# Row maximum and scaling of attention scores in one VectorE operation, with the threshold kept in PSUM

## Chip, cores and metric

The program runs on one core of a Trainium2 chip. The metric is device time in microseconds (us) of one execution; lower is better. The names of the engines are those of the profile: PE (TensorE), DVE (VectorE), ACT (ScalarE), POOL (GpSimd) and SP, whose queue issues most DMAs.

## What is computed

Attention with a threshold, then a mixture of experts over its output. The change lies in the attention alone (batch 8, heads 8, sequence 576, head dimension 64):

```
scale = 1.0 / np.sqrt(q.shape[-1])                       # 0.125
scores = scale * np.matmul(q, k.transpose(0, 1, 3, 2))
thresh = np.max(scores, axis=-1, keepdims=True) - tau
scores = np.where(scores >= thresh, scores, -1000000000.0)
scores = scores - np.max(scores, axis=-1, keepdims=True)
attn = np.exp(scores)
attn = attn / (np.sum(attn, axis=-1, keepdims=True) + 1e-09)
out = np.matmul(attn, v)
```

Then each token of the output whose `x @ w_skip` is positive goes to the one of 8 experts with the highest gate value: `x + gate * (relu(x @ w1[e]) @ w2[e])`. Everything is fp32.

## The kernel before

Queries are taken in tiles of 128 rows. A group `g` is two heads of one batch (32 groups); it has 9 items (`STEP`): four query tiles of each head, and one item for the two remainders of 64 rows together. So 288 items run through the same steps, with their names in `plan_item`:

- `score` (PE, L686): two fp32 matmuls of 288 columns each, into two adjacent PSUM banks. Three such pairs are in use at a time (`SPB`), and a pair comes free only after `mask`.
- `top` (DVE, L691): the row maximum over the 576 scores, read from PSUM, into `mx[..0]`.
- `small` (DVE, L695): from the maximum, two numbers per row in one scalar_tensor_tensor whose two tensor inputs, `cd` and `cd` again, lie in SBUF: `max - 8*tau` (the threshold on unscaled scores) and `-0.125*max` (the bias).
- `expo` (ACT, L700): `exp(0.125*score + bias)` from PSUM into `p` in SBUF.
- `mask` (DVE, L706): `(score >= threshold) * p`, with the scores from PSUM and `p` from SBUF.

After the two items of a query tile, `fph` makes an fp16 copy `pk` of `p` (ACT or DVE, L510/L512), `fpl` the fp16 remainder (POOL, L737), and SP transposes `pk` by DMA into `pt` or `ptm`. PE then multiplies these by the values (L788, L792), a sum column gives the normalizer, POOL scales (L841), and PE and DVE work out the gate logits.

The order of all this on every engine is written by a planner (`Plan`): each step is given as an operation with its dependences, a due time and a cost, and the planner simulates the engines and sorts; a list of seeds (`SEEDS`) disturbs the order, and the last disturbed order is emitted. Where the planner sees PE idle, it puts in matmuls without use (`fill`, L518), as many as fit into the share `FILL` of the gap. An engine takes its instructions strictly in the order that was emitted. After the attention (up to about 750 us) come the experts, PE with weights streamed in, whose code isn't touched.

Of the kernel before, what the change touches and what calls it, by code (L numbers as in the profile page):

```python
# [12 lines left out]
F32 = mybir.dt.float32  # L13
# [4 lines left out]
AF = mybir.ActivationFunctionType  # L18
ALU = mybir.AluOpType
AX = mybir.AxisListType  # L20
# [4 lines left out]
P = 128  # L25
S = 576
# [8 lines left out]
HS = S // 2  # L35
# [15 lines left out]
STEP = 2 * NM + 1  # L51
NBK = 2 * NM + 1
SPB = 3
FILL = 0.7
SHB = 2
QB = 3
PFB = 4
# [21 lines left out]
SHARED = {"shp": 0, "gps": 0, "avp": 0, "sps": 2}  # L79
BANKS = 8  # L80
SEEDS = (
# [6 lines left out]
)  # L88
DLAT = 0.7
OFF = dict(  # L90
    ld=14.0, S=3.0, mx=2.4, sm=2.3, e=2.0, p=1.6, ph=0.6, phD=3.0, pl=0.4, tr=0.0, av=3.0, v=24.0, v0=20.0, ldv=-6.0, vsp=1.0, ld0=-30.0,
    init=6.0, row=2.0, rsp=0.5, L1=4.0, sc=0.0,
)

# [43 lines left out]
class Plan:  # L138
# [4 lines left out]
    def emit(self, o):  # L143
# [6 lines left out]
        if e == "PE" and o.real and o.idle[1] is not None:  # L150
            for _ in range(int(FILL * o.idle[0] / 0.115)):
                self.fill(o.idle[1])
# [218 lines left out]
def attn_moe_kernel(ctx: ExitStack, tc: tile.TileContext, qk, vl, tau, wg, w1, w2, out):  # L371
    nc = tc.nc
# [5 lines left out]
    cp = ctx.enter_context(tc.tile_pool(name="cp", bufs=1))  # L378
# [18 lines left out]
    taue = cp.tile([P, 1], F32, name="taue")  # L397
    nc.scalar.activation(taue, cnt[:, 0:1], AF.Exp)
    nc.vector.tensor_scalar(taue, taub, 0.0, None, op0=ALU.max)
    cd = cp.tile([P, 4], F32, name="cd")  # L400
    nc.gpsimd.memset(cd[:, 0:1], 1.0)
    nc.gpsimd.memset(cd[:, 1:2], -0.125)
    nc.gpsimd.memset(cd[:, 3:4], 0.0)
    nc.vector.tensor_scalar(cd[:, 2:3], taue, -8.0, None, op0=ALU.mult)
    jt = cp.tile([P, P], F32R, name="jt")
    onesr = cp.tile([1, P], F32, name="onesr")

# [77 lines left out]
    pl = Plan(tc)  # L485
    PE, DVE, ACT, POOL, SPQ = "PE", "DVE", "ACT", "POOL", "SP"
    BOTH = (DVE, POOL)

    def wtile(dt, name, n=1):
        return wraw.tile([P, n * WW], dt, name=name, tag="wr")  # L490
# [17 lines left out]
    def copy(e, dst, src):  # L508
        if e == ACT:
            nc.scalar.activation(dst, src, AF.Copy)  # L510
        else:
            nc.vector.tensor_copy(dst, src)  # L512

    ring = pl
# [6 lines left out]
    T = {}  # L521
# [143 lines left out]
    def sps():  # L665
        a, b = pl.bank
        return banks[:, a : b + 1 : b - a]

    def plan_item(g, i):
        n = STEP * g + i  # L670
        M = i == STEP - 1
        c, h = divmod(i, 2)
        ends = M or h == 1
        z = ("p", g, c)
        items = 1 if M else 2

        def two(t):
            return t.rearrange("p (a b) -> p a b", a=2)

        def score():  # L680
            T["S", g, i] = ps = sps()
            raw = T["raw", g]
            rs = slice(0, P) if M else slice(h * D, h * D + D)
            for j in range(2):
                ks = slice(QW + j * HS, QW + j * HS + HS)
                nc.tensor.matmul(ps[:, j, 0:HS], raw[rs, c * P : c * P + P], raw[rs, ks], start=True, stop=True)  # L686

        def top():
            if i == 0:
                T["mx", g] = ap_.tile([P, STEP, 4], F32, name="mx", tag="mx", bufs=3)  # L690
            nc.vector.tensor_reduce(T["mx", g][:, i, 0:1], T["S", g, i][:, :, 0:HS], AX.XY, ALU.max)  # L691

        def small():
            m = T["mx", g][:, i]
            nc.vector.scalar_tensor_tensor(m[:, 1:3], cd[:, 0:2], m[:, 0:1], cd[:, 2:4], op0=ALU.mult, op1=ALU.add)  # L695

        def expo():
            if h == 0:
                T[z] = ap_.tile([P, 2, S], F32, name="p", tag="p", bufs=PFB)
            nc.scalar.activation(  # L700
                two(T[z][:, h]), T["S", g, i][:, :, 0:HS], AF.Exp, bias=T["mx", g][:, i, 2:3], scale=0.125
            )

        def mask():
            e = two(T[z][:, h])
            nc.vector.scalar_tensor_tensor(  # L706
                e, T.pop(("S", g, i))[:, :, 0:HS], T["mx", g][:, i, 1:2], e, op0=ALU.is_ge, op1=ALU.mult
            )

        s = pl.op(n - OFF["S"], score, [T["q", g]] + ring.take("sps", SPB), {PE: 1.05 if M else 0.56})  # L710
        m = pl.op(n - OFF["mx"], top, [s] + (ring.take("mx", 3) if i == 0 else [T["m0", g]]), {DVE: 0.665})
        if i == 0:
            T["m0", g] = m
        m = pl.op(n - OFF["sm"], small, [m], {DVE: 0.13})
        e = pl.op(n - OFF["e"], expo, [m] + (ring.take("p", PFB) if h == 0 else T["es", g]), {ACT: 0.635})
        x = pl.op(n - OFF["p"], mask, [e], {DVE: 0.725})
        ring.free("sps", [x])
        T.setdefault(("Sop", g), []).append(s)
        T.setdefault(("es", g), []).append(e)
        T.setdefault(("ms", g), []).append(x)  # L720
        T.setdefault(("all", g), []).append(x)
        if M:
            ring.free("raw", T["Sop", g])
            ring.free("mx", T["all", g])
        if not ends:
            return
        ms, T["ms", g], T["es", g] = T["ms", g], [], []

        def fph(e):
            T["k", g, c] = ap_.tile([P, 2, 2 * S], F16, name="pk", tag="pk", bufs=KB)  # L730
            copy(e, T["k", g, c][:, 0:items, 0:S], T[z][:, 0:items])

        def fpl():
            k, p = T["k", g, c][:, 0:items], T.pop(z)[:, 0:items]
            for lo, w, at in ((0, NM * P, S + TL), (NM * P, TL, S)):
                ks = slice(lo, lo + w)
                nc.gpsimd.tensor_tensor(k[:, :, at : at + w], p[:, :, ks], k[:, :, ks], op=ALU.subtract)  # L737

        def turn():
            k = T.pop(("k", g, c))  # L740
            if M:
                T["pt", g, c] = PTM[g % MB]
                nc.sync.dma_start_transpose(T["pt", g, c][:, :, TL : TL + P], k[:, 0])
                return
            if c % 2 == 0:
                T["slot", g, c // 2] = wtile(F16, "pt", 2).rearrange("p (c a k q) -> p c a k q", c=2, a=2, q=P)
            T["pt", g, c] = pt = T["slot", g, c // 2][:, c % 2]
            nc.sync.dma_start_transpose(pt.rearrange("p a k q -> p (a k) q"), k.rearrange("p a b -> p (a b)"))

        w = items * S  # L750
        ph = pl.op(
            n - OFF["ph"],
            fph,
            ms + ring.take("pk", KB),
            {ACT: w / 1160 + 0.1, DVE: w / 1920 + 0.12},
            off={DVE: OFF["phD"]},
            port=BOTH,
        )
        lo = pl.op(n - OFF["pl"], fpl, [ph], {POOL: w * 0.00206 + 0.12})
        ring.free("p", [lo])  # L760
        q = ring.take("ptm", MB) if M else ring.take("wr", WRB) if c % 2 == 0 else [(T["tr", g, c - 1],)]
        t = T["tr", g, c] = pl.dma(n - OFF["tr"], turn, [ph, lo] + q, [0.35], 1.35 * items)
        ring.free("pk", [t])
        if M:
            for hd in range(2):
                plan_av(g, hd, n)
# [727 lines left out]
    for g in range(NG):  # L1494
        if g + 2 < NG:
            plan_load(g + 2)
        for i in range(STEP):
            t = STEP * g + i
            plan_item(g, i)
            while later and later[0][0] <= t:  # L1500
                later.pop(0)[1]()
        if g % HP == HP - 2 and g + 2 < NG:
            plan_v(g // HP + 1)
# [404 lines left out]
```

## Time and profile before

| | |
|---|---|
| runs before, median (lowest to highest) | 1059.12 us (1057.99 to 1062.39), 3 runs |
| the profiled execution's own time | 1049.39 us |
| its span, first to last instruction | 1047.6 us |
| granted TensorE clock, mean over the span | 0.905 |
| busy: PE, DVE, ACT, POOL | 93%, 74%, 55%, 59% of the span |

[...] PE's busy share contains the fill matmuls. All durations of the rows below come from the one profiled execution, which is about 10 us under the median of the three runs.

### The profile page before, as it was taken

How to read it: one execution, taken by the hardware profiler on the slowest of the kernel's cores; microseconds unless marked ns; L12 is line 12 of the kernel's file. 1: busy time of each engine (PE TensorE's matmuls, PEld its weight loads, DVE VectorE, ACT ScalarE, POOL GpSimd, SP SyncE). 2: the span in 40 equal slices, each digit the busy share in tenths (PEclk: the TensorE clock that was granted, in tenths of full speed). 3: DMA queues.
4: the chain of work that ended last, by engine and by line, in shares of the span. 5: the costliest groups of instructions: out<-in, count | busy, mean ns of one | idle time of the engine just before them, and what ended most of it. 6: DMA issues, size and time to landing. Idle time of an engine off the chain costs nothing. (4 is left out here: it accounts for less than half of the span.)

```text
span 1047.6 us, 21896 instructions
## 1 busy us (share of the span) xinstructions
PE 973.9 (93%) x8602; PEld 746.1 (71%) x8602; DVE 774.9 (74%) x1376; ACT 579.6 (55%) x872; POOL 617.8 (59%) x566
## 2 busy tenths in 40 slices
PE   7998999998989899899999999999988999999995
PEld 4666666766666676666656776666777989999994
DVE  7988698698679897968986788978645455557771
ACT  4766566666565676557656657645422434434450
POOL 4666575575466476656866576767715446444461
PEclk9999799699789898969987889977989999999998
DMA  6899697799579779958996689876943655344530
GB/s 177 170 194 151 119 234 155 131 208 202 106 160 177 177 143 229 182 105 165 181 207 140 152 202 167 156 156 116 191 152 124 214 181 160 129 164 175 191 126 17
DMA packets 371817, 169.79 MB, mean 162 GB/s; under 512 B 344270, under 2 KB 344270, under 8 KB 371712
## 3 DMA queue, kind: packets, MB, share of 16 engines
q1 hardware_dynamic: 367024, 158.72, 69.4%
q0 software_dynamic: 4544, 9.65, 2.9%
q8 instruction: 68, 1.11, 0.4%
q14 instruction: 37, 0.30, 0.1%
q10 hardware_dynamic: 144, 0.00, 0.0%
HBM read 69.46 MB, written 15.21 MB: 81 GB/s over the span
## 5 line engine op out<-in xcount | busy, mean ns | idle before, releaser
L737 POOL TENSOR_TENSOR pk<-p,pk 128x1024 f16<-128x1024 f32 (+1 forms) x320 | 366.8, 1170 | 230.6 <-issue 113.4
L686 PE MATMUL banks<-raw 64*128 64x288 f32 (+1 forms) x1152 | 377.4, 472 | 34.2 <-DVE p L706 32.1
L700 ACT ACTIVATE p<-banks,mx 128x576 f32<-128x576 f32 x288 | 210.2, 737 | 187.1 <-DVE mx L695 157.4
L691 DVE TENSOR_REDUCE mx<-banks 128x1 f32<-128x576 f32 x288 | 215.2, 751 | 113.6 <-PE banks L686 110.4
L686 PEld LDWEIGHTS banks<-raw 64*128 64x128 f32 (+1 forms) x1152 | 202.0, 207 | 115.0 <-DVE p L706 48.0
L706 DVE SCALAR_TENSOR_TENSOR p<-banks,mx,p 128x576 f32<-128x576 f32 x288 | 230.1, 807 | 8.6 <-ACT p L700 7.6
L510 ACT ACTIVATE pk<-p 128x1152 f16<-128x1152 f32 (+1 forms) x154 | 164.2, 1067 | 32.3 <-DVE p L706 21.0
L695 DVE SCALAR_TENSOR_TENSOR mx<-cd,mx 128x2 f32<-128x2 f32 x288 | 178.7, 625 | 2.4
L788 PEld LDWEIGHTS <-pt 128*128 128x128 f16 x2304 | 128.8, 104 | 26.7 <-issue 24.4
L518 PE MATMUL banks<-jt 128*128 128x256 f16 x874 | 138.3, 296 | 3.3 <-DVE p L706 2.2
L792 PE MATMUL banks<-Vl,pt 128*128 128x64 f16 x1280 | 139.2, 201 | 1.2 <-POOL Vl L645 1.2
L788 PE MATMUL banks<-Vh,pt 128*128 128x65 f16 x2304 | 139.8, 203 | 0.0
L518 PEld LDWEIGHTS <-jt 128*128 128x128 f16 x874 | 82.9, 105 | 68.7 <-issue 57.3
L792 PEld LDWEIGHTS <-pt 128*128 128x128 f16 x1280 | 122.8, 105 | 3.2 <-issue 0.5
L1542 POOL TENSOR_TENSOR wl<-wr,wh 128x1024 fp32r<-128x1024 f32 x28 | 72.4, 2603 | 35.3 <-ACT wh L1541 29.9
L1581 PE MATMUL hps<-xh,wl 128*128 128x256 f32 (+4 forms) x256 | 77.0, 301 | 0.0
L1581 PE MATMUL hps<-xh,wh 128*128 128x256 f32 (+4 forms) x248 | 76.4, 308 | 0.0
L1581 PE MATMUL hps<-xl,wh 128*128 128x256 f32 (+4 forms) x248 | 75.0, 302 | 0.0
L1582 ACT ACTIVATE HH<-hps 128x256 fp32r<-128x256 f32 (+4 forms) x64 | 27.0, 422 | 68.4 <-PE hps L1581 67.8
L1593 POOL DMA_INDIRECT out<-o,ids x21 | 21.1, 1006 | 72.0 <-DVE o L1592 28.9
L1541 ACT ACTIVATE wh<-wr 128x1024 fp32r<-128x1024 f32 x60 | 60.6, 1050 | 0.0
L1583 DVE SCALAR_TENSOR_TENSOR HH<-hps,HH 128x256 fp32r<-128x256 f32 (+4 forms) x64 | 31.1, 487 | 39.0 <-ACT HH L1582 38.9
(211 smaller groups left out, 1303.8 us busy)
## 6 DMA issues: line engine op xcount, KB each, us to landing
wr<-in_w SPq DMA_DIRECT2D x30, 1024.0 KB, 5.4
raw<-in_qk SPq DMA_DIRECT2D x32, 608.0 KB, 4.8
vraw<-in_vl SPq DMA_DIRECT2D x32, 320.0 KB, 4.2
out<-xb SPq DMA_DIRECT2D x32, 256.0 KB, 2.7
pt<-pk SPq DMA_TRANSPOSE x128, 5.2
rw<-in_w SPq DMA_DIRECT2D x2, 1024.0 KB, 6.4
out<-x SPq DMA_DIRECT2D x8, 128.0 KB, 2.8
lst<-rec,si POOLq DMA_INDIRECT x36, 3.9
```

The costliest lines, as they stand in the source:

```text
L510: nc.scalar.activation(dst, src, AF.Copy)
L518: nc.tensor.matmul(banks[:, n, 0 : 2 * P], x[:, 0:P], x[:, 0 : 2 * P], start=True, stop=True, skip_group_check=True)
L686: nc.tensor.matmul(ps[:, j, 0:HS], raw[rs, c * P : c * P + P], raw[rs, ks], start=True, stop=True)
L691: nc.vector.tensor_reduce(T["mx", g][:, i, 0:1], T["S", g, i][:, :, 0:HS], AX.XY, ALU.max)
L695: nc.vector.scalar_tensor_tensor(m[:, 1:3], cd[:, 0:2], m[:, 0:1], cd[:, 2:4], op0=ALU.mult, op1=ALU.add)
L700: nc.scalar.activation(two(T[z][:, h]), T["S", g, i][:, :, 0:HS], AF.Exp, bias=T["mx", g][:, i, 2:3], scale=0.125)
L706: nc.vector.scalar_tensor_tensor(e, T.pop(("S", g, i))[:, :, 0:HS], T["mx", g][:, i, 1:2], e, op0=ALU.is_ge, op1=ALU.mult)
L737: nc.gpsimd.tensor_tensor(k[:, :, at : at + w], p[:, :, ks], k[:, :, ks], op=ALU.subtract)
L788: nc.tensor.matmul(pv[:, c, :], x, Vh[:, vh, kt, :], start=(c + kt + i == 0), stop=False, skip_group_check=True)
L792: nc.tensor.matmul(pv[:, c, 0:D], x, Vl[:, vh, kt, :], start=False, stop=last, skip_group_check=True)
L1542: lo[q % 2].tensor_tensor(w[1][:, sl], rs, w[0][:, sl].bitcast(F32), op=ALU.subtract)
L1581: nc.tensor.matmul(hp_[:, 0:cap], w_, x, start=(i == 0), stop=(i == len(mm) - 1))
```

## The change

`top` becomes one tensor_tensor_reduce: it adds a zero tile, broadcast from one element in SBUF, to the scores, multiplies by -0.125, writes the result back over the scores in PSUM, and reduces by minimum with the accumulator output `mx[..1]`. That minimum is `-0.125*max`, so it is the bias of `expo` directly, and `expo` scales by -1. `small` becomes `minimum + tau`, one element per row, written to PSUM beside the scores (column 288 of the first bank), and `mask` compares with `<=` against it there. The planner's table changes with it: `expo` depends on `top` and no longer on `small`; `mask` depends on both. `FILL` goes from 0.7 to 0.5, and the seeds are others. The constants `cd` go, and a memset of one zero comes.

```
-FILL = 0.7
+FILL = 0.5
...
-    ld=14.0, S=3.0, mx=2.4, sm=2.3, e=2.0, p=1.6, ph=0.6, phD=3.0, pl=0.4, tr=0.0, av=3.0, v=24.0, v0=20.0, ldv=-6.0, vsp=1.0, ld0=-30.0,
+    ld=14.0, S=3.0, mx=2.4, th=2.1, e=2.0, p=1.6, ph=0.6, phD=3.0, pl=0.4, tr=0.0, av=3.0, v=24.0, v0=20.0, ldv=-6.0, vsp=1.0, ld0=-30.0,
...
-            nc.vector.tensor_reduce(T["mx", g][:, i, 0:1], T["S", g, i][:, :, 0:HS], AX.XY, ALU.max)
+            y = T["S", g, i][:, :, 0:HS]
+            nc.vector.tensor_tensor_reduce(
+                y, y, zero.broadcast_to([P, 2, HS]), -0.125, 3.0e38, ALU.add, ALU.min, T["mx", g][:, i, 1:2]
+            )
...
-            m = T["mx", g][:, i]
-            nc.vector.scalar_tensor_tensor(m[:, 1:3], cd[:, 0:2], m[:, 0:1], cd[:, 2:4], op0=ALU.mult, op1=ALU.add)
+            nc.vector.tensor_scalar(T["S", g, i][:, 0, HS : HS + 1], T["mx", g][:, i, 1:2], taue, None, op0=ALU.add)
...
-                two(T[z][:, h]), T["S", g, i][:, :, 0:HS], AF.Exp, bias=T["mx", g][:, i, 2:3], scale=0.125
+                two(T[z][:, h]), T["S", g, i][:, :, 0:HS], AF.Exp, bias=T["mx", g][:, i, 1:2], scale=-1.0
...
-                e, T.pop(("S", g, i))[:, :, 0:HS], T["mx", g][:, i, 1:2], e, op0=ALU.is_ge, op1=ALU.mult
+                e, ps[:, :, 0:HS], ps[:, 0, HS : HS + 1], e, op0=ALU.is_le, op1=ALU.mult
...
-        m = pl.op(n - OFF["sm"], small, [m], {DVE: 0.13})
-        e = pl.op(n - OFF["e"], expo, [m] + (ring.take("p", PFB) if h == 0 else T["es", g]), {ACT: 0.635})
-        x = pl.op(n - OFF["p"], mask, [e], {DVE: 0.725})
+        y, m = m, pl.op(n - OFF["th"], small, [m], {DVE: 0.13})
+        e = pl.op(n - OFF["e"], expo, [y] + (ring.take("p", PFB) if h == 0 else T["es", g]), {ACT: 0.635})
+        x = pl.op(n - OFF["p"], mask, [m, e], {DVE: 0.725})
```

What the built program makes of it on DVE, in the order of its queue, in the first third of the attention (`[waits X]` names the engine whose semaphore the instruction waits for; Activation is ACT). Before, three scores were reduced with their `small` steps between, and every `mask` waited for ACT:

```order
L706 SCALAR_TENSOR_TENSOR p<-banks,mx,p 128x576 [waits Activation_49]
L833 RECIPROCAL z<-z 128x10 [waits Activation_49]
L691 TENSOR_REDUCE mx<-banks 128x1 [waits PE_49]
L706 SCALAR_TENSOR_TENSOR p<-banks,mx,p 128x576 [waits Activation_49]
L695 SCALAR_TENSOR_TENSOR mx<-cd,mx 128x2 [waits DVE_49]
L691 TENSOR_REDUCE mx<-banks 128x1 [waits PE_49] x2
L695 SCALAR_TENSOR_TENSOR mx<-cd,mx 128x2 [waits DVE_49]
```

Of the change, near the same place (lines move by 8 to 10 up to L716, so `top` is L700, `small` L705, `expo` L710, `mask` L716):

```order
L716 SCALAR_TENSOR_TENSOR p<-banks,p 128x576 [waits Activation_49]
L700 ISA banks,mx<-banks,zero 128x2x288 [waits PE_49]
L700 ISA mx 128x1
L843 RECIPROCAL z<-z 128x10 [waits Activation_49]
L705 TENSOR_SCALAR banks<-mx,taue 128x1 [waits Activation_49]
L700 ISA banks,mx<-banks,zero 128x2x288 [waits PE_49]
L700 ISA mx 128x1
L716 SCALAR_TENSOR_TENSOR p<-banks,p 128x576 [waits DVE_49,Pool_49]
L705 TENSOR_SCALAR banks<-mx,taue 128x1 [waits Activation_49]
L705 TENSOR_SCALAR banks<-mx,taue 128x1 [waits DVE_49]
L716 SCALAR_TENSOR_TENSOR p<-banks,p 128x576 [waits DVE_49]
```

The one tensor_tensor_reduce is two DVE instructions, the pass over the scores and one that writes out the accumulator (`ISA mx`). `small` has moved behind the exponential in 157 of the 288 items: there it waits for ACT, since it writes into the bank that `expo` reads; in the others `expo` waits for it. In 70 places a `small` that waits for ACT stands directly in front of another `small`.

On PE, at the transpose for the value maximum of the fourth batch (`ident,vmx`), before; `jt` are the fill matmuls and `raw` the scores:

```order
L593 MATMUL banks<-ident,vmx 1x128 [waits DVE_49]
L686 MATMUL banks<-raw 128x288 [waits DVE_49]
L686 MATMUL banks<-raw 128x288
L518 LDWEIGHTS jt
L518 MATMUL banks<-jt 128x256 [waits Activation_49]
L686 MATMUL banks<-raw 128x288 [waits DVE_49]
```

Of the change:

```order
L601 MATMUL banks<-ident,vmx 1x128 [waits DVE_49]
L694 MATMUL banks<-raw 128x288 [waits DVE_49]
L694 MATMUL banks<-raw 128x288
L526 LDWEIGHTS jt
L526 MATMUL banks<-jt 128x256 [waits Activation_49]
L526 LDWEIGHTS jt
L526 MATMUL banks<-jt 128x256
L694 MATMUL banks<-raw 128x288 [waits DVE_49]
```

The fill matmuls stand at other places, and over the whole program there are 578 of them, where before there were 874. The number of DMAs and of POOL operations on data is the same in both.

## Rows read from the trace of the kernel before

**Rows 1.** Page, head: span of the profiled execution and its instructions

```profile
span 1047.6 us, 21896 instructions
```

**Rows 2.** Busy us by engine in two stages: attention and experts

```profile
core 0: us, PE busy (x) PEld busy (x) DVE busy (x) ACT busy (x) POOL busy (x), PEclk, DMA share, GB/s
0.00:750.00 750.00, 699.21 (x6640) 492.76 (x6641) 612.82 (x1111) 467.01 (x682) 480.09 (x475) 0.88 0.83 167
750.00:1048.00 298.00, 274.67 (x1962) 253.31 (x1961) 162.13 (x266) 112.56 (x191) 137.75 (x92) 0.96 0.46 149
```

**Rows 3.** Groups by line in 0 to 750 us: busy us, mean ns | idle before

```profile
L706 DVE SCALAR_TENSOR_TENSOR p<-banks,mx,p 128x576 f32<-128x576 f32 x288 | 230.1, 807 | 8.6 <-ACT p L700 7.6
L691 DVE TENSOR_REDUCE mx<-banks 128x1 f32<-128x576 f32 x288 | 215.2, 751 | 113.6 <-PE banks L686 110.4 <-ACT z L830 0.7 <-ACT p L700 0.5
L695 DVE SCALAR_TENSOR_TENSOR mx<-cd,mx 128x2 f32<-128x2 f32 x288 | 178.7, 625 | 2.4
...
L518 PE MATMUL banks<-jt 128*128 128x256 f16 x845 | 134.3, 296 | 3.3 <-DVE p L706 2.2 <-DVE lg L937 1.1
```

**Rows 4.** Waits in 0 to 750 us: total us, times, longest us

```profile
ACT p L700 <- DVE mx L695: 157.4, 118, 4.5
...
DVE mx L691 <- PE banks L686: 110.4, 112, 3.6
...
PEld banks L686 <- DVE p L706: 48.0, 55, 2.3
PE banks L686 <- DVE p L706: 32.1, 42, 2.1
```

**Rows 5.** Tile mx: ns min/median/max of its instructions

```profile
L695 DVE SCALAR_TENSOR_TENSOR mx<-cd,mx x288: 187/308/3793, 10.4 to 748.4; 128x2 f32<-128x2 f32 x144
...
L706 DVE SCALAR_TENSOR_TENSOR p<-banks,mx,p x288: 743/808/820, 11.6 to 749.7; 128x576 f32<-128x576 f32 x144
```

**Rows 6.** Timeline of DVE around 325 us: start us, length us

```profile
324.26 0.80 DVE L706 SCALAR_TENSOR_TENSOR p<-banks,mx,p 128x576 f32<-128x576 f32 x1
324.99 2.17 DVE L695 SCALAR_TENSOR_TENSOR mx<-cd,mx 128x2 f32<-128x2 f32 x1
```

**Rows 7.** Timeline of POOL in 324 to 327 us

```profile
325.01 2.13 POOL L737 TENSOR_TENSOR pk<-p,pk 128x1024 f16<-128x1024 f32 x1 [1.34 <-issue]
```

**Rows 8.** Timeline of all engines, 363.5 to 370 us

```profile
363.80 1.68 DVE L695 SCALAR_TENSOR_TENSOR mx<-cd,mx 128x2 f32<-128x2 f32 x1
...
365.40 2.25 DVE L706 SCALAR_TENSOR_TENSOR p<-banks,mx,p 128x576 f32<-128x576 f32 x3
365.57 0.74 ACT L700 ACTIVATE p<-banks,mx 128x576 f32<-128x576 f32 x1 [2.31 <-DVE mx L695]
...
366.26 1.23 PE L686 MATMUL banks<-raw 64*128 64x288 f32 x4 [1.76 <-DVE p L706]
```

**Rows 9.** Timeline of POOL in 364 to 365.4 us

```profile
363.34 2.12 POOL L737 TENSOR_TENSOR pk<-p,pk 128x1024 f16<-128x1024 f32 x1
```

**Rows 10.** Small DVE instructions by line: ns min/median/max

```profile
L598 DVE TENSOR_SCALAR vmx<-vmx x8: 141/142/143, 19.5 to 642.5; 1x1 f32<-1x1 f32 x8
L1039 DVE TENSOR_SCALAR gw<-gw x5: 158/161/336, 230.1 to 781.2; 128x9 f32<-128x9 f32 x3, 128x4 f32<-128x4 f32 x1, 128x5 f32<-128x5 f32 x1
L833 DVE RECIPROCAL z<-z x32: 194/205/216, 60.3 to 768.3; 128x10 f32<-128x10 f32 x32
```

**Rows 11.** Two-input DVE operations with (L1030) and without (L1102) a broadcast input

```profile
L1030 DVE TENSOR_TENSOR ca<-lg,gw x5: 181/223/224, 226.9 to 780.6; 128x72 f32<-128x72 f32 x3, 128x32 f32<-128x32 f32 x1, 128x40 f32<-128x40 f32 x1
L1102 DVE TENSOR_TENSOR ca<-ca x5: 186/232/233, 348.6 to 784.1; 128x72 f32<-128x72 f32 x3, 128x32 f32<-128x32 f32 x1, 128x40 f32<-128x40 f32 x1
```

**Rows 12.** Groups by line and shape: one DVE operation at two widths

```profile
L1583 DVE SCALAR_TENSOR_TENSOR HH<-hps,HH 128x256 fp32r<-128x256 f32 x24 | 10.1, 419 | 14.5 <-ACT HH L1582 14.5
...
L1583 DVE SCALAR_TENSOR_TENSOR HH<-hps,HH 128x384 fp32r<-128x384 f32 x8 | 4.4, 553 | 7.4 <-ACT HH L1582 7.4
```

**Rows 13.** Fill matmuls (L518) alone in stretches: busy us and count, granted clock

```profile
350.00:400.00 50.00, 8.50 (x59) 4.97 (x59) 1.00 0.79 155
450.00:500.00 50.00, 9.92 (x59) 5.83 (x60) 0.85 0.67 129
...
700.00:750.00 50.00, 16.02 (x97) 10.04 (x97) 0.83 0.82 156
```

More of the change, by code (lines that the diff above doesn't have):

```diff
@@ L399, in attn_moe_kernel @@
     nc.vector.tensor_scalar(taue, taub, 0.0, None, op0=ALU.max)
[L400 to L404, printed above, removed]
+    zero = cp.tile([P, 1, 1], F32, name="zero")
+    nc.vector.memset(zero, 0.0)
     jt = cp.tile([P, P], F32R, name="jt")
@@ L700, in expo @@
             nc.scalar.activation(
-                two(T[z][:, h]), T["S", g, i][:, :, 0:HS], AF.Exp, bias=T["mx", g][:, i, 2:3], scale=0.125
+                two(T[z][:, h]), T["S", g, i][:, :, 0:HS], AF.Exp, bias=T["mx", g][:, i, 1:2], scale=-1.0
             )
         def mask():
-            e = two(T[z][:, h])
+            e, ps = two(T[z][:, h]), T.pop(("S", g, i))
             nc.vector.scalar_tensor_tensor(
-                e, T.pop(("S", g, i))[:, :, 0:HS], T["mx", g][:, i, 1:2], e, op0=ALU.is_ge, op1=ALU.mult
+                e, ps[:, :, 0:HS], ps[:, 0, HS : HS + 1], e, op0=ALU.is_le, op1=ALU.mult
             )
         s = pl.op(n - OFF["S"], score, [T["q", g]] + ring.take("sps", SPB), {PE: 1.05 if M else 0.56})
-        m = pl.op(n - OFF["mx"], top, [s] + (ring.take("mx", 3) if i == 0 else [T["m0", g]]), {DVE: 0.665})
+        m = pl.op(n - OFF["mx"], top, [s] + (ring.take("mx", 3) if i == 0 else [T["m0", g]]), {DVE: 0.73})
         if i == 0:
             T["m0", g] = m
-        m = pl.op(n - OFF["sm"], small, [m], {DVE: 0.13})
-        e = pl.op(n - OFF["e"], expo, [m] + (ring.take("p", PFB) if h == 0 else T["es", g]), {ACT: 0.635})
-        x = pl.op(n - OFF["p"], mask, [e], {DVE: 0.725})
+        y, m = m, pl.op(n - OFF["th"], small, [m], {DVE: 0.13})
+        e = pl.op(n - OFF["e"], expo, [y] + (ring.take("p", PFB) if h == 0 else T["es", g]), {ACT: 0.635})
+        x = pl.op(n - OFF["p"], mask, [m, e], {DVE: 0.725})
         ring.free("sps", [x])
```

23 rows, old and new, of the table SEEDS are left out of this document.

## The prediction

> **What bounds the kernel now.** I read the stages first. The profiled execution spans 1047.6 us [rows 1] and took 1049.4; in the attention, its first 750 us, PE is busy for 699 us, DVE for 613, ACT for 467, POOL for 480 and the DMA engines for a share of 0.83 [rows 2]. The change touches only this stage; the experts' 298 us stay. Per item (288 of them) the stage takes 2.60 us. DVE works 613 / 288 = 2.13 us of it. PE works 699 - 134 = 565 us without its fill matmuls [rows 3], 1.96 us an item, and is idle for only 750 - 699 = 51 us. So no engine is full with real work; PE and DVE hand an item to and fro and wait for each other. The list of waits shows both directions: `top` waited 110 us for scores, and the scores' weight loads waited 48 us (the matmuls 32 us of the same moments) for a `mask` that frees a PSUM pair; ACT waited 157 us for `small`, but ACT has room [rows 4].
>
> Then I looked at DVE's three steps. `top` takes 751 ns and `mask` 807. `small`, two elements a row, takes 625 ns in the mean [rows 3], from 187 ns at best to 3793 ns at worst [rows 5]. The timelines tell why: at 324.99 us a `small` lasts 2.17 us, to 327.16, and POOL's subtraction, begun at 325.01, ends at 327.14 [rows 6, 7]; at 363.80 another lasts until 365.48, and POOL's ends at 365.46 [rows 8, 9]. A DVE operation with two inputs from SBUF is held until POOL's is done. `mask`, with one input from PSUM and one from SBUF, never goes over 820 ns beside the same POOL work [rows 5], so it isn't held.
>
> **The change part by part.**
>
> Removed: the holds. An unheld `small` is near 0.21 us (best 0.187), so of the 178.7 us, 178.7 - 288 x 0.21 = 118 us are holds [rows 3, 5]. The new `small` has one tensor input in SBUF and writes PSUM, and the new `top` reads one input from PSUM and one from SBUF as `mask` does; I expect neither to be held. Whether they are hasn't been seen: the bounds are -118 us and 0.
>
> Added on DVE. The new `top` also writes 576 elements to PSUM, which no row shows. Lower bound: the reduction's 751 ns. Nearest row: `mask`, same inputs and width, 807. Upper bound: if reading and writing one bank took turns, the columns would count twice; a column costs (553 - 419) / 128 = 1.05 ns [rows 12], so 576 x 1.05 = 0.60 us or 174 us in all. I take `mask`: 288 x 0.056 = +16 us. The broadcast zero costs nothing: an operation with a broadcast input took 223 ns, one without 232 [rows 11]. The accumulator's write is an instruction more per item; between nothing and the 205 ns of a small reciprocal, I take the 0.13 to 0.14 of a one-element operation [rows 10]: 288 x 0.13 = +37 us. Bare `small` goes from 0.21 to the 0.16 of a small tensor_scalar [rows 10]: -14 us. Net on DVE: -118 + 16 + 37 - 14 = -79 us.
>
> [...]
>
> Not all of this reaches the end. An evenly spread microsecond of DVE counts where PE waits for DVE and not where DVE waits for PE: 48 / (48 + 110) = 0.30 [rows 4]. A hold comes in one piece and hits harder: the one at 363.80 made the masks behind it late, and PE stood 1.76 us and ACT 2.31 [rows 8]. I take 0.4 for holds (chosen, between 0.30 and 1) and 0.3 for the rest: -118 x 0.4 = -47, and (16 + 37 - 14) x 0.3 = +12.
>
> Moved: `small` behind `expo`, 157 times. Before, it stood in front of `expo`; the work on the item's path stays about equal. But in the 70 places where a second `small` follows one that waits for ACT, the second item's exponential starts only when the first is done and both `small` steps behind it: 2 x 0.16 plus two hand-offs of 0.09 (365.48 to 365.57 [rows 8]) = 0.5 us, 35 us in all; queued behind are the next `top` and the `mask` that frees the pair for PE. Most of ACT's wait is covered by its idle time; without that cover it costs the 35. At 0.3: +10.
>
> Fill matmuls: 296 fewer, each 134.3 / 845 = 0.16 us [rows 3], 47 us of PE. They stand in gaps and cost only where a score is ready behind them. If they lie evenly, the 110 of 750 us in which DVE waits for scores are what counts, 15%: -7 (bounds 0 and -47).
>
> The single memset at the start replaces four others, and costs nothing. SP's and POOL's queues issue the same transfers; with the stage some 4% shorter the DMA share goes from 0.83 to about 0.87, so I price no new wait there.
>
> Sum: -47 + 12 + 10 - 7 = -32 us. From the profiled 1049.4 that is 1017; this execution lies 10 us under the median of the runs, 1059.1, so the forecast for the median is 1027, rounded to **1028 us**.
>
> **The rivals.**
>
> *More on the path.* If nearly every hold and fill delays PE, the gain is bounded by what PE has to give: its 51 us idle and the 7 of the fills, 58 us: 1001. For it: DVE is so close to full between waits that PE's idle time is mostly DVE's making. Against: DVE itself waited 110 us for scores [rows 4], which a faster DVE doesn't shorten.
>
> *No change.* The write to PSUM costs what the holds gave. It decides at 79 / 288 = 0.27 us over my price: `top` and its accumulator together 0.41 us longer than the reduction. Or the new `small` is held as the old was. Time 1059. Against: no row puts a DVE pass of this width over 820 ns; for it: none writes PSUM.
>
> [...]
>
> **How the numbers follow.** Forecast (1012 to 1048): 0.50. More on the path (995 to 1012): 0.15. No change: 0.16, which includes gains eaten in part. Slower: 0.19. A change of 0.5% (5 us) is about what a measurement of this kernel can tell from none. So faster 0.66, same 0.15, slower 0.19: the no-change case spills 0.01 over. The range 1000 to 1066 leaves out the lower part of the second case and most of the slower one, about 2 in 10.
>
> **What would show it.** The new `small` under 0.25 us with no value in the thousands, and no pile-up at the ends of POOL's L737; `top` near 0.81 and the accumulator near 0.13; DVE's busy time in the attention near 613 - 79 = 534 us; the last `mask`, now at 750 us, near 718; the clock in that stage between 0.85 and 0.90; and ACT waiting for `small` in place of `top` where two stand together. Wrong it would be if `top` goes to 1.1 us or more, if holds turn up in it, if the clock falls under 0.83, or if the scores wait longer for `mask` because `small` stands on ACT.

## The result, and the profile after

| | before | changed |
|---|---|---|
| runs, median (lowest to highest) | 1060.72 us (1057.99 to 1062.39), 4 runs | 975.81 us (962.80 to 988.07), 4 runs |
| ratio, with its 95% interval | | 0.9108 (0.9045 to 0.9171) |
| the profiled execution's own time | 1049.39 us | 982.69 us |
| granted TensorE clock, mean over the span | 0.905 | 0.901 |

By the ratio, the change makes the kernel 8.9% faster, 95 us of 1061; the medians of the table differ by 85 us. The forecast was 1028 us, and the range from 1000 to 1066 doesn't hold the result. The ratio leaves out runs at a lower granted clock; the profiled execution is one of them (the four runs had clocks of 0.901, 0.921, 0.896 and 0.924, and times of 982.69, 968.92, 988.07 and 962.80 us), so its rows compare structure, not the last per cent.

The stages of the changed kernel, busy us by engine, for [rows 2]; the last `mask` now ends at 680 us:

```profile
core 0: us, PE busy (x) PEld busy (x) DVE busy (x) ACT busy (x) POOL busy (x), PEclk, DMA share, GB/s
0.00:681.00 681.00, 647.26 (x6453) 455.95 (x6453) 505.73 (x1393) 469.85 (x685) 474.71 (x469) 0.88 0.93 181
681.00:981.00 300.00, 273.26 (x1855) 251.23 (x1853) 160.17 (x267) 112.84 (x191) 141.61 (x95) 0.96 0.48 156
```

The attention takes 681 us in place of 750, at the same granted clock of 0.88; the experts take 300 in place of 298. DVE's busy time falls by 107 us, while ACT and POOL do the work they did. The DMA share rises from 0.83 to 0.93, more than the 0.87 forecast.

Groups by line in that stage (busy us, mean ns | idle before), for [rows 3]:

```profile
L716 DVE SCALAR_TENSOR_TENSOR p<-banks,p 128x576 f32<-128x576 f32 x288 | 232.6, 817 | 9.2 <-ACT p L710 6.9
L700 DVE CUSTOM_DVE_ANT_1 banks<-banks,zero 128x576 f32<-128x576 f32 x288 | 218.2, 765 | 123.9 <-PE banks L694 122.1 <-issue 1.0
...
L526 PE MATMUL banks<-jt 128*128 128x256 f16 x531 | 88.9, 292 | 2.7 <-ACT a L518 1.3 <-DVE p L716 0.8 <-DVE tab L1222 0.5
L705 DVE TENSOR_SCALAR banks<-mx,taue 128x1 f32<-128x1 f32 x288 | 57.8, 217 | 29.4 <-ACT p L710 27.1
...
L700 DVE DVE_READ_ACCUMULATOR2_ANT mx<- 128x1 f32 x288 | 40.8, 142 | 0.0
```

`small` went from 178.7 us to 57.8. The new `top` takes 765 ns where the reduction took 751, and the fills shrank from 134.3 us to 88.9. The tile `mx` (min/median/max ns), for [rows 5], shows that no `small` is held any more: the longest of 288 takes 224 ns, where it was 3793:

```profile
L700 DVE DVE_READ_ACCUMULATOR2_ANT mx<- x288: 129/142/144, 9.3 to 678.1; 128x1 f32 x144
L705 DVE TENSOR_SCALAR banks<-mx,taue x288: 158/220/224, 9.5 to 679.2; 128x1 f32<-128x1 f32 x144
```

The waits of the stage (total us, times, longest us), for [rows 4]:

```profile
DVE banks L700 <- PE banks L694: 122.1, 139, 3.7
...
ACT p L710 <- DVE mx L700: 49.3, 45, 3.0
...
ACT p L710 <- DVE banks L705: 45.1, 48, 3.0
ACT pk L518 <- DMA pt<-pk: 35.8, 26, 4.6
...
DVE banks L705 <- ACT p L710: 27.1, 44, 3.2
PEld banks L694 <- DVE p L716: 24.6, 38, 1.7
...
PE banks L694 <- DVE p L716: 12.5, 20, 1.4
```

The scores' waits for `mask` are half of what they were (weight loads 48.0 to 24.6, matmuls 32.1 to 12.5), and `top` waits more for scores (110.4 to 122.1). ACT's wait for DVE fell from 157.4 to 49.3 + 45.1 = 94.4. ACT also waits 35.8 us to overwrite a `pk` whose transposing DMA is still under way. Before, that wait was 4.6 us:

```profile
ACT pk L510 <- DMA pt<-pk: 4.6, 6, 1.3
```

One thing has to be seen before the busy times are compared. The timeline of DVE (start us, length us) in the changed kernel:

```profile
299.47 0.77 DVE L700 CUSTOM_DVE_ANT_1 banks<-banks,zero 128x576 f32<-128x576 f32 x1 [0.94 <-PE banks L694]
300.15 0.14 DVE L700 DVE_READ_ACCUMULATOR2_ANT mx<- 128x1 f32 x1
300.15 0.80 DVE L700 CUSTOM_DVE_ANT_1 banks<-banks,zero 128x576 f32<-128x576 f32 x1
300.87 0.14 DVE L700 DVE_READ_ACCUMULATOR2_ANT mx<- 128x1 f32 x1
300.87 0.80 DVE L700 CUSTOM_DVE_ANT_1 banks<-banks,zero 128x576 f32<-128x576 f32 x1
```

The accumulator's read starts in the same moment as the next pass (in 228 of the 288 cases it starts together with another DVE instruction), and each pass starts some 0.08 us before the one ahead of it ends (300.15 + 0.80 = 300.95, the next at 300.87). The records of DVE overlap, for the reads in 37.6 of their 40.8 us. Here a short instruction therefore takes less of DVE's time than its own duration says; what counts is the engine's busy time in a window, where overlaps are counted once.

### The profile page after: what moved, and what is told of

Same layout as the page of the kernel before. It is cut to its first block, busy times and chain, and to the rows that moved or that the text cites. A ratio compares the mean times of both kernels' runs of the same rounds, so it can differ in the third digit from the quotient of the medians.

```text
span 980.9 us, 21639 instructions
## 1 busy us (share of the span) xinstructions
PE 920.5 (94%) x8306; PEld 707.2 (72%) x8306; DVE 665.9 (68%) x1660; ACT 582.7 (59%) x876; POOL 616.3 (63%) x563
## 5 line engine op out<-in xcount | busy, mean ns | idle before, releaser
L694 PE MATMUL banks<-raw 64*128 64x288 f32 (+1 forms) x1152 | 366.0, 476 | 15.6 <-DVE p L716 12.5
L700 DVE CUSTOM_DVE_ANT_1 banks<-banks,zero 128x576 f32<-128x576 f32 x288 | 218.2, 765 | 123.9 <-PE banks L694 122.1
L710 ACT ACTIVATE p<-banks,mx 128x576 f32<-128x576 f32 x288 | 210.2, 737 | 107.0 <-DVE mx L700 49.3
L694 PEld LDWEIGHTS banks<-raw 64*128 64x128 f32 (+1 forms) x1152 | 199.2, 208 | 94.6 <-DVE p L716 24.6
L716 DVE SCALAR_TENSOR_TENSOR p<-banks,p 128x576 f32<-128x576 f32 x288 | 232.6, 817 | 9.2 <-ACT p L710 6.9
L518 ACT ACTIVATE pk<-p 128x1152 f16<-128x1152 f32 (+1 forms) x158 | 168.3, 1065 | 49.9 <-DMA pt<-pk 37.9
L798 PEld LDWEIGHTS <-pt 128*128 128x128 f16 x2304 | 132.5, 105 | 25.8 <-issue 22.7
L798 PE MATMUL banks<-Vh,pt 128*128 128x65 f16 x2304 | 143.0, 205 | 1.9 <-issue 1.9
L802 PEld LDWEIGHTS <-pt 128*128 128x128 f16 x1280 | 124.7, 106 | 3.5 <-issue 1.8
L526 PE MATMUL banks<-jt 128*128 128x256 f16 x578 | 95.0, 292 | 2.9 <-ACT a L518 1.3
L526 PEld LDWEIGHTS <-jt 128*128 128x128 f16 x578 | 51.9, 103 | 56.1 <-issue 49.5
L705 DVE TENSOR_SCALAR banks<-mx,taue 128x1 f32<-128x1 f32 x288 | 57.8, 217 | 29.4 <-ACT p L710 27.1
L518 ACT ACTIVATE a<-banks 128x325 f32<-128x325 f32 x64 | 28.0, 438 | 52.9 <-PE banks L802 39.0
```

The source lines that it names most:

```text
L526: nc.tensor.matmul(banks[:, n, 0 : 2 * P], x[:, 0:P], x[:, 0 : 2 * P], start=True, stop=True, skip_group_check=True)
L700: nc.vector.tensor_tensor_reduce(y, y, zero.broadcast_to([P, 2, HS]), -0.125, 3.0e38, ALU.add, ALU.min, T["mx", g][:, i, 1:2])
L710: nc.scalar.activation(two(T[z][:, h]), T["S", g, i][:, :, 0:HS], AF.Exp, bias=T["mx", g][:, i, 1:2], scale=-1.0)
L716: nc.vector.scalar_tensor_tensor(e, ps[:, :, 0:HS], ps[:, 0, HS : HS + 1], e, op0=ALU.is_le, op1=ALU.mult)
L798: nc.tensor.matmul(pv[:, c, :], x, Vh[:, vh, kt, :], start=(c + kt + i == 0), stop=False, skip_group_check=True)
L802: nc.tensor.matmul(pv[:, c, 0:D], x, Vl[:, vh, kt, :], start=False, stop=last, skip_group_check=True)
```

## The experiments

The forecast counted 32 us; 95 came. Three theories: **H**, the holds of `small` cost PE more than the 0.4 us per us that the forecast took. **F**, the fills that were taken out stood in front of real scores, and their 45 us came back in full. **O**, the new order (other seeds, `expo` no longer behind `small`) is better by itself. Gains below are differences of ratios to the kernel before, times 1061 us, with the two intervals combined as independent ones. A loss against the changed kernel that is worked out so is some 10 us larger than the difference of the medians would be (1061 x 0.9108 = 966, its median 976).

**Fills put back, and taken out of the kernel before.** F is tried from both sides.

```
# e1_after_fill07: the changed kernel
-FILL = 0.5
+FILL = 0.7
# e2_before_fill05: the kernel before
-FILL = 0.7
+FILL = 0.5
```

> The changed kernel with the share of the fill matmuls put back to 0.7: 858 fill matmuls in place of 578, every other instruction in the same order. If the fewer fills gave most of the gain (theory F), about 45 us of PE time comes back and the time is 1000 to 1015 us. If the holds of small did (theory H), or the new order did (theory O), the time stays within 10 us of the changed kernel, 960 to 985.

> The kernel before with the fill share at 0.5: 597 fills in place of 874, the rest as before. F: 1015 to 1030 us, a third or more of the 90 us. H and O: within 10 us of before, 1050 to 1065.

With 858 fills in place of 578 the changed kernel took 977.69 us, ratio 0.9248 (0.9112 to 0.9385), not told apart from 0.9108. The kernel before with 597 fills in place of 874 took 1069.74 us, 1.0122 (0.9987 to 1.0257): no gain. Its attention (first window) in the profile:

```profile
0.00:777.00 777.00, 714.04 (x6404) 497.34 (x6405) 606.93 (x1111) 467.84 (x683) 480.08 (x476) 0.82 0.80 162
```

The granted clock of that stage is 0.82, where it was 0.88 [rows 2]; both are means (in windows of 2 us of the trace before it is 1.00 from 424 to 442 us and 0.50 from 446 to 458). F falls as the cause of the gain: fewer fills don't make the kernel before faster, and putting them back costs the changed kernel 15 ± 16 us of the 95. That the time of the fills is free doesn't follow. The scores' matmuls in the attention before, and the scores' and the fills' with 597 fills:

```profile
L686 PE MATMUL banks<-raw 64*128 64x288 f32 (+1 forms) x1152 | 377.4, 472 | 34.2 <-DVE p L706 32.1 <-ACT a L510 1.8
```

```profile
L686 PE MATMUL banks<-raw 64*128 64x288 f32 (+1 forms) x1152 | 400.4, 502 | 45.7 <-DVE p L706 43.8 <-ACT a L510 1.3 <-DVE raw L538 0.4
...
L518 PE MATMUL banks<-jt 128*128 128x256 f16 x576 | 102.4, 305 | 3.2 <-DVE p L706 1.8 <-DVE lg L937 1.3
```

The fills take 32 us less, but at the lower clock the same scores take 502 ns for 472, and all of PE's other work 714.0 - 102.4 = 612 us where it took 565. What fewer fills free and what the clock takes back happen at once; these runs show only that the sum is no gain.

**Fewer still.** Does the granted clock follow the fills?

```
# e8_after_fill03: the changed kernel
-FILL = 0.5
+FILL = 0.3
```

> The changed kernel with the fill share at 0.3, 318 fills for 578. If fills cost PE time, 965 us or less; if they hold up the clock, the granted clock falls under 0.90 and the time rises to 980 to 1000.

986.53 us, 0.9354 (0.9253 to 0.9455): 26 ± 13 us slower than the changed kernel. The attention of this kernel, and then of the one with 0.7, each with its scores and fills:

```profile
0.00:684.00 684.00, 642.57 (x6225) 451.78 (x6226) 506.41 (x1393) 469.97 (x685) 474.40 (x469) 0.84 0.91 180
...
L694 PE MATMUL banks<-raw 64*128 64x288 f32 (+1 forms) x1152 | 375.4, 484 | 21.9 <-DVE p L716 19.8 <-DVE raw L546 0.9 <-ACT a L518 0.6
...
L526 PE MATMUL banks<-jt 128*128 128x256 f16 x303 | 58.3, 297 | 4.4 <-DVE p L716 3.6 <-ACT a L518 0.8
```

```profile
0.00:684.00 684.00, 664.68 (x6695) 471.71 (x6696) 508.09 (x1393) 470.00 (x685) 474.71 (x468) 0.90 0.93 180
...
L694 PE MATMUL banks<-raw 64*128 64x288 f32 (+1 forms) x1152 | 358.8, 461 | 13.1 <-DVE p L716 11.6 <-ACT a L518 0.7 <-ACT vmx L628 0.2
...
L526 PE MATMUL banks<-jt 128*128 128x256 f16 x786 | 124.8, 295 | 0.0
```

The order of real work is the same in both, and with 318, 578 and 858 fills the attention's clock is 0.84, 0.88 and 0.90 (over the span, all runs: 0.865 to 0.880, 0.896 to 0.928 and 0.920 to 0.940). In these three kernels the fills raise the granted clock, and from 578 to 858 of them this no longer shows in the time (975.81 and 977.69 us): with 58, 89 and 125 us of fills, PE's other work in the attention takes 584, 558 and 540 us.

**The holds alone, taken away and put back.** In the kernel before, with its order, `small` becomes two operations with one SBUF tensor each. In the changed kernel, the new `small` gets a second SBUF tensor input, its result still going to PSUM.

```
# e3_before_no_hold: the kernel before
-            nc.vector.scalar_tensor_tensor(m[:, 1:3], cd[:, 0:2], m[:, 0:1], cd[:, 2:4], op0=ALU.mult, op1=ALU.add)
+            nc.vector.tensor_scalar(m[:, 1:2], m[:, 0:1], cd[:, 2:3], None, op0=ALU.add)
+            nc.vector.tensor_scalar(m[:, 2:3], m[:, 0:1], -0.125, None, op0=ALU.mult)
# e4_after_hold: the changed kernel
-            nc.vector.tensor_scalar(T["S", g, i][:, 0, HS : HS + 1], T["mx", g][:, i, 1:2], taue, None, op0=ALU.add)
+            nc.vector.scalar_tensor_tensor(
+                T["S", g, i][:, 0, HS : HS + 1], T["mx", g][:, i, 1:2], 1.0, taue, op0=ALU.mult, op1=ALU.add
+            )
```

> The kernel before, in its own order, with small as two tensor_scalar instructions of one SBUF input each in place of the one with two SBUF inputs: the holds should go (no small over 0.35 us), for one more DVE instruction per item, about 0.14 us. H: 990 to 1015 us, the larger half of the gain. F and O: 1045 to 1065, since order and fills are those of before.

> The changed kernel with small as an operation of two SBUF inputs (tau added as a tensor input) and the same result, so that POOL can hold it again; order and fills are those of the change. H: small's mean goes from 0.2 to about 0.6 us, and the time to 1020 to 1050. F and O: within 15 us of the changed kernel, 960 to 990.

Without holds the kernel before took 993.51 us, 0.9406 (0.9264 to 0.9548): 63 ± 15 us gained, with one operation more per item and the order and fills of before. Its tile `mx`, and its attention, which ends at 699 us, with `top`'s wait for scores and the fills:

```profile
L695 DVE TENSOR_SCALAR mx<-mx,cd x288: 151/206/216, 10.4 to 696.7; 128x1 f32<-128x1 f32 x144
L696 DVE TENSOR_SCALAR mx<-mx x288: 130/144/148, 10.5 to 696.8; 128x1 f32<-128x1 f32 x144
```

```profile
0.00:699.00 699.00, 676.63 (x6657) 481.52 (x6658) 516.37 (x1399) 467.52 (x681) 479.32 (x475) 0.90 0.90 179
...
DVE mx L691 <- PE banks L686: 157.1, 176, 3.1
...
L518 PE MATMUL banks<-jt 128*128 128x256 f16 x845 | 129.8, 289 | 0.4 <-DVE p L707 0.4
```

DVE's busy time fell by 612.8 - 516.4 = 96 us [rows 2], and `top` now waits 157.1 us for scores, where it waited 110.4: of what DVE gave, a part turned into waiting for PE. The granted clock rose as well, from 0.88 to 0.90 in the attention, and PE's work without fills fell from 565 to 676.6 - 129.8 = 547 us: some 18 of the 51 us by which the attention is shorter.

With holds the changed kernel took 1023.30 us, 0.9653 (0.9453 to 0.9853): 58 ± 22 us lost. Its `small` (tile view), DVE and POOL at one of the holds, and its attention with the scores' waits for `mask`:

```profile
L705 DVE SCALAR_TENSOR_TENSOR banks<-mx,taue x288: 143/202/4642, 9.5 to 722.3; 128x1 f32<-128x1 f32 x144
```

```profile
260.73 2.17 DVE L705 SCALAR_TENSOR_TENSOR banks<-mx,taue 128x1 f32<-128x1 f32 x2
```

```profile
260.69 2.12 POOL L749 TENSOR_TENSOR pk<-p,pk 128x1024 f16<-128x1024 f32 x1
```

```profile
0.00:724.00 724.00, 672.96 (x6462) 475.45 (x6463) 582.28 (x1393) 469.90 (x686) 474.75 (x469) 0.85 0.85 170
...
PEld banks L694 <- DVE p L718: 47.7, 58, 4.2
...
PE banks L694 <- DVE p L718: 30.1, 35, 3.8
```

The holds are back (median 202 ns, longest 4642): two of these one-element operations last until 262.90, and POOL's subtraction ends at 262.81. This is so throughout the attention: counted in the traces, all 78 of its `small` steps that last over 0.5 us end 23 to 35 ns behind the end of a POOL operation, and all 104 of the kernel before 8 to 27 ns behind one. PE's waits are back too, 47.7 and 30.1, as they were before [rows 4]. DVE's busy time in the attention rose by 77 us, to 582.3, and the granted clock fell from 0.88 to 0.85. H holds, from both sides: some 60 of the 95 us, with what the clock adds included. In the changed kernel the longest `small` takes 224 ns without the second SBUF tensor input and 4642 with it; in the kernel before, 216 without it and 3793 with it.

**Is it the holds, or any time on DVE?** The same sort of time is added evenly (a memset of 192 columns behind each `top`) and in lumps (one of 1024 columns ahead of `small` in every third item).

```
# e6_after_extra_dve: the changed kernel, behind the tensor_tensor_reduce; scr is a tile of 192 columns
+            nc.vector.memset(scr, 0.0)
# e9_after_lumps: the changed kernel, ahead of small's tensor_scalar; scr has 1024 columns
+            if i % 3 == 1:
+                nc.vector.memset(scr, 0.0)
```

> The changed kernel with a memset of 192 columns behind every top, about 0.25 us of DVE for each of the 288 items, 72 us in all, which nothing needs. If even DVE time counts in full on this stage (the removed 78 us of the second run before gave 68), 1030 to 1050 us; if it counts at 0.3, as the prediction took it, 990 to 1005; if only stalls in one piece count, under 990.

> The changed kernel with a memset of 1024 columns ahead of small in every third item: 96 pieces of about 0.9 us, 87 us in all, as many and as long as the holds that the kernel with the two-input small showed (88 of 0.97 us in the mean, 85 us), but at fixed places and not tied to what POOL does. If one-piece stalls of DVE cost what they cost wherever they fall, 1010 to 1035 us, as with the holds; if holds cost more because they come while POOL works on the remainder, 980 to 1000; even DVE time of that sum gave 7 to 17 us.

The even memsets: 982.56 us, 0.9292 (0.9205 to 0.9379), 20 ± 11 us lost by the ratios; the time lies where only stalls in one piece were to count. The lumps: 1009.58 us, 0.9495 (0.9382 to 0.9608), 41 ± 14 us lost. The attention of the first and then of the second, and their memsets by line:

```profile
0.00:682.00 682.00, 649.52 (x6460) 460.51 (x6461) 543.30 (x1681) 473.31 (x685) 474.51 (x469) 0.87 0.92 180
...
L704 DVE MEMSET scr<- 128x192 f32 x288 | 62.8, 218 | 0.0
```

```profile
0.00:703.00 703.00, 656.38 (x6422) 461.57 (x6423) 574.05 (x1485) 470.22 (x685) 473.71 (x467) 0.88 0.90 175
...
L707 DVE MEMSET scr<- 128x1024 f32 x96 | 87.6, 912 | 16.0 <-issue 7.3 <-DVE banks L708 3.1 <-DVE p L719 0.7
```

The even memsets of 62.8 us raised DVE's busy time by only 543.3 - 505.7 = 37.6 us, since each overlaps its neighbours; the lumps of 87.6 raised it by 68.3. Per microsecond of busy time, then, even time costs 20 / 37.6 = 0.53, lumps 41 / 68.3 = 0.60, and holds 63 / 96 = 0.65 (taken away) or 58 / 77 = 0.75 (put back). The intervals (0.53 ± 0.29, 0.75 ± 0.29) don't separate these, so that a hold hurts more than the same time elsewhere isn't shown. Nor is it shown that even time costs anything. The runs with even memsets had clocks of 0.900 to 0.903 and took 979.24 to 985.80 us; the changed kernel's own runs at 0.896 to 0.902, two of the first four and two of e11 below, took 982.69 to 988.07. The runs with lumps lie above these at a like clock: 1005.35 us at 0.901.

**The order alone.** The changed kernel is planned with the seeds of before; and the changed kernel keeps its order on every engine, instruction by instruction, but has the old arithmetic, without a hold and with the threshold in SBUF.

```
# e7_after_old_seeds: the changed kernel, with the tuple SEEDS of the kernel before (647 fills)
# e10_old_ops_new_order: the changed kernel; tau8 is -8 * taue, worked out once
-            nc.vector.tensor_tensor_reduce(
-                y, y, zero.broadcast_to([P, 2, HS]), -0.125, 3.0e38, ALU.add, ALU.min, T["mx", g][:, i, 1:2]
-            )
+            nc.vector.tensor_reduce(m[:, 0:1], T["S", g, i][:, :, 0:HS], AX.XY, ALU.max)
+            nc.vector.tensor_scalar(m[:, 1:2], m[:, 0:1], -0.125, None, op0=ALU.mult)
...
-            nc.vector.tensor_scalar(T["S", g, i][:, 0, HS : HS + 1], T["mx", g][:, i, 1:2], taue, None, op0=ALU.add)
+            nc.vector.tensor_scalar(T["mx", g][:, i, 2:3], T["mx", g][:, i, 0:1], tau8, None, op0=ALU.add)
...
-bias=T["mx", g][:, i, 1:2], scale=-1.0
+bias=T["mx", g][:, i, 1:2], scale=0.125
...
-e, ps[:, :, 0:HS], ps[:, 0, HS : HS + 1], e, op0=ALU.is_le, op1=ALU.mult
+e, ps[:, :, 0:HS], T["mx", g][:, i, 2:3], e, op0=ALU.is_ge, op1=ALU.mult
```

> The changed kernel planned with the seeds of before: the same operations in another, less searched order, with 647 fills. If the new seeds are a part of the gain (theory O in a smaller form), 985 to 1010 us; if the order hardly matters, within 10 us of the changed kernel, 965 to 985.

> The changed kernel's order on every engine and its fills, but the old arithmetic: a row maximum (nothing is written back to PSUM), a one-element multiply by -0.125 for the bias, and small as one addition with one SBUF input, threshold in SBUF. No hold, as many DVE instructions as the changed kernel. If the new operation itself gives anything, 985 to 1000 us, like the old order without holds (993); if only the end of the holds and the order count, 955 to 975, like the changed kernel with the threshold in SBUF.

> The changed kernel as it is, beside the other two on the same chip, since its runs so far lay between 963 and 988 us: by every theory 960 to 990, and its own granted clock to set beside theirs.

With the old seeds: 998.96 us, 0.9430 (0.9332 to 0.9527), 34 ± 12 us behind the changed kernel and beside the 0.9406 of the kernel before without holds. With the old arithmetic in the new order: 980.41 us, 0.9181 (0.9078 to 0.9284); the changed kernel itself, on the same chip as this one, 979.55 us, 0.9108 (0.8978 to 0.9237). These two are not told apart (8 ± 18 us); 980.41 lies between the two ranges expected. The attention and the tile `mx` of the old arithmetic:

```profile
0.00:680.00 680.00, 648.30 (x6390) 455.87 (x6391) 527.89 (x1389) 468.97 (x684) 472.35 (x465) 0.87 0.92 180
...
L700 DVE TENSOR_REDUCE mx<-banks x288: 696/757/759, 9.0 to 679.1; 128x1 f32<-128x576 f32 x144
L701 DVE TENSOR_SCALAR mx<-mx x288: 153/154/155, 9.8 to 679.8; 128x1 f32<-128x1 f32 x144
L704 DVE TENSOR_SCALAR mx<-mx,tau x288: 151/204/209, 9.8 to 680.6; 128x1 f32<-128x1 f32 x144
```

O holds for some 24 (0.9406 - 0.9181, ± 19) to 34 us, the other numbers of fills included (874 and 578 in the one pair, 647 and 578 in the other). The operation in the title saves DVE 22 us (505.7 for 527.9), but gives no time beyond this that these runs can tell.

**The threshold in SBUF.** `small` writes to `mx[..2]` in place of PSUM, and `mask` reads it there; the order stays, but `small` no longer shares a bank with `expo`.

```
# e5_thresh_sbuf and e12_thresh_sbuf_again: the changed kernel
-            nc.vector.tensor_scalar(T["S", g, i][:, 0, HS : HS + 1], T["mx", g][:, i, 1:2], taue, None, op0=ALU.add)
+            nc.vector.tensor_scalar(T["mx", g][:, i, 2:3], T["mx", g][:, i, 1:2], taue, None, op0=ALU.add)
...
-                e, ps[:, :, 0:HS], ps[:, 0, HS : HS + 1], e, op0=ALU.is_le, op1=ALU.mult
+                e, ps[:, :, 0:HS], T["mx", g][:, i, 2:3], e, op0=ALU.is_le, op1=ALU.mult
```

> The changed kernel with the threshold written to SBUF and not beside the scores in PSUM: the order is the same, but small shares no bank with the exponential, so that neither waits for the other. If the waits between small and the exponential (27 us of DVE, 45 us of ACT in the changed kernel's list) are on the path as the prediction's term of +10 us had it, 960 to 970 us; if they are covered by what follows, 970 to 985, the changed kernel's own time.

> The changed kernel with the threshold in SBUF once more, in five rounds, since its four runs (961 to 966) lay at the lower end of the changed kernel's eight (962 to 988). If it is the better version, all runs stay under 970 and the ratio to before under 0.91; if the two are alike, it shows runs of 980 to 988 as well and a ratio of 0.91 to 0.92.

963.61 us, 0.9117 (0.9036 to 0.9197), and in six more runs 971.89 us, 0.9132 (0.9051 to 0.9213): by the ratios as the changed kernel. The waits between the two, in the first of these:

```profile
DVE p L716 <- ACT p L710: 20.0, 25, 4.0
ACT p L710 <- DVE mx L705: 14.9, 18, 2.7
```

`small` itself no longer waits for ACT (27.1 us in the changed kernel), ACT waits 14.9 us for it in place of 45.1, and `mask` waits for ACT 20.0 us in place of 6.9. At like clocks, this version is the faster one by a little: 977.64 against 982.69 us at 0.901, 971.66 against 975.22 at 0.911, 957.52 against 962.80 at 0.924, and 961.25 to 966.09 for the first four runs, at 0.910 to 0.914. So the waits may cost some 4 to 14 us; the chips differ, and it isn't settled. This version differs from the old arithmetic above in `top` alone, and 0.9117 and 0.9132 beside 0.9181 (5 to 7 us, ± 14) don't show a gain of the new operation either. By the ratios no version here beats the changed kernel.

## Why the prediction was wrong

The direction was right, and so was the mechanism of the holds; the forecast gain was a third of the measured one. By its steps:

- **"Removed: the holds"**: right. No `small` above 224 ns, and the holds return with a second SBUF tensor input (longest 4642). `small` fell by 178.7 - 57.8 = 121 us against the 118 + 14 forecast, for holds and bare work.
- **The write to PSUM, "I take `mask`: +16 us"**: too high. `top` takes 765 ns, 14 more than the reduction, 4 us in all, and the broadcast zero, forecast at nothing, is within these 14.
- **The accumulator, "+37 us"**: its duration was right (142 ns, 40.8 us in all), its effect wasn't. By lines DVE's change is -121 + 3 + 41 + 2 (`mask`, 232.6 for 230.1) = -75 us, near the -79 forecast; by the engine's busy time it is -107. The 32 between them is about what the reads share with the instruction beside them (counted in the trace, 37.6 of their 40.8 us). What a read costs is then an estimated (41 - 32) / 288, some 31 ns, where the forecast took 130.
- **"I take 0.4 for holds and 0.3 for the rest"**: the first step that failed. The 0.3 came from dividing PE's wait for DVE by the sum of both waits [rows 4]; for holds the runs give 0.65 (63 us for 96) and 0.75 (58 for 77) per us of DVE's busy time. Taking the holds away was worth 63 ± 15 us by itself, where the sum had 47 and took 12 off again. A part of this comes through the granted clock, which the forecast's sum had at nothing: 0.88 to 0.90 when the holds go, 0.88 to 0.85 when they are put back. For even time, 0.3 is neither borne out nor refuted.
- **The order**: the second step that failed. Moving `small` was priced at +10 us and the rest of the new plan at nothing. The +10 may be about right (4 to 14 us at like clocks, not told by the ratios), but the plan as a whole gains 24 to 34 us. With the 63 of the holds that makes 87 to 97 of the 95 us, and each term is uncertain by 12 to 19.
- **The fills, "-7"**: no net effect on the time that shows, while the granted clock follows them. Their time and the clock pull against each other: with 597 fills in the kernel before, PE's other work grew by 47 us while the fills shrank by 32. The forecast's sum has the time of the fills alone. In [rows 13] 59 fills go with a clock of 1.00 and with one of 0.85; those were stretches of one kernel with different real work. With the real work the same, 318, 578 and 858 fills give 0.84, 0.88 and 0.90. The chance of 0.19 for slower: the changed kernel's attention keeps the 0.88 of before with 578 fills, and no run of it is slower than before; the kernel before with fewer fills fell to 0.82, at a ratio of 1.0122 (0.9987 to 1.0257).
- **The cap of the rival "more on the path", 58 us**: wrong as a bound. It gave PE only its 51 us of idle time and 7 of the fills. Fills stand where PE has nothing to do, so all of the 134 us belong to the idle time: 750 - 565 = 185 us. PE used 69 of them without being busier with real work (647 - 89 = 558 us, before 565).
- **The rival "no change", 0.41 us**: a slip in the sum. `top` and its accumulator would have to be 0.056 + 0.13 + 0.27 = 0.46 us longer than the reduction. They are 0.014 + 0.142 = 0.16 us longer, far from either.
- **"No new wait" on the DMAs**: not so. ACT waits 35.8 us for `pk` to be read, where it waited 4.6. What this costs wasn't tried.

Open: what in the new plan makes it better, the freed dependence of `expo` or the seeds chosen for it (those of before were not chosen for this plan); what even DVE time costs, and so whether a hold costs more; and how much of the fills' time would come back at an unchanged clock.

## What to carry to other kernels

An operation of two elements per row can be the most expensive small thing in a loop (here 178.7 us, the longest 3793 ns beside a median of 308): look at the largest value beside the median, and at what POOL does in that moment; one input fewer from SBUF took this away with plain operations (none above 216 ns), and the cleverer single operation wasn't needed. When bounding what a kernel can gain, count filler matmuls as idle time, but fewer of them can lower the granted clock and slow the real work by as much as they free (277 fewer in the kernel before: the clock from 0.88 to 0.82, 32 us freed, PE's other work 47 us longer); and weigh DVE by its busy time in a window, not by the sum of its records (-107 us here, by the records -75). Set runs side by side at like granted clocks before a difference of 20 us is given a cause. Where a change also brings a newly searched order, price the order as a term with its own bounds, and run the old arithmetic in the new order to tell the two apart.

## What was not expected of the hardware

- The accumulator's read of 142 ns starts together with another VectorE instruction in 228 of 288 cases, and neighbouring records overlap by some 0.08 us.
- The pass that also writes 576 elements per row back to PSUM takes 765 ns, 14 more than the reduction that doesn't.
- A VectorE instruction of two elements per row with two SBUF inputs was held until POOL's operation ended: 104 of 288 lasted over 0.5 us, and every one of these ended within 27 ns of POOL's.
- With the same real work, the granted clock of the attention was 0.84, 0.88 and 0.90 with 318, 578 and 858 fills, and the same score matmuls took 484, 476 and 461 ns in the mean. The runs of the changed kernel differ among themselves (962.80 to 988.07 us) as their clocks do (0.924 to 0.896).
